# Block-sparse attention with a gated FFN on one Trainium2 core: which tensor goes through the crossbar DMA, q and k of three batches or the normalised attention output

## Chip, core and metric

The kernel runs on one core of a Trainium2 chip. The metric is device time in microseconds (us) of one execution; less is better. The kernel before takes 306.27 us, the median of three runs (305.6 to 307.56).

## What is computed

Attention over 4 batches, 8 heads, 768 tokens and 64 elements a head, with a mask of 32x32 blocks (first and last block row and column, the diagonal and its neighbours, three sampled blocks a row), and then a gated FFN over the 3072 tokens:

```python
scores = scale * np.matmul(q, k.transpose(0, 1, 3, 2))
...
scores = np.where(mask, scores, -1000000000.0)
...
attn = attn / (np.sum(attn, axis=-1, keepdims=True) + 1e-09)
return np.matmul(attn, v).astype(np.float32)
...
x = np.ascontiguousarray(attn_out.transpose(0, 2, 1, 3)).reshape(B * S, H * D)
...
gate = 1.0 / (1.0 + np.exp(-(x @ w_gate)))
val = x @ w_val
return (gate * val @ w_out).astype(np.float32)
```

x is 3072x512; w_gate and w_val are 512x1536, w_out is 1536x512. Inputs and output are float32; the kernel computes on float16.

## The kernel before, in words

**Units.** The work is cut into 12 units, numbered n (L601): batch b from 0 to 3, and within a batch three runs of 256 query tokens, u from 0 to 2. In each unit the 8 heads are taken as 4 pairs p (class `Pair`), two heads of 64 elements filling 128 partitions. A pair has 3 steps (class `Step`), each of 256 keys: scores on TensorE (L406, into one of two PSUM tiles of kind "s"), exp on ScalarE (L416), a product with the mask on VectorE (L422). Then come the product with v (L445, 24 matmuls into one of four PSUM banks of kind "m"; a column of ones in `vex` gives the row sums), and `norm` on VectorE (L455, L457), which divides and writes `x16`, 128 tokens by (2 token tiles, 2 heads, 64).

**x^T.** The FFN wants x with its 512 columns on the partitions. So each pair's `x16` is turned: `turn` (L464) makes two 128x128 transposes on TensorE into an "m" bank, and `evac` (L472) copies the bank into `xT` (four buffers, `XB`) on VectorE or ScalarE. `Pair.xt` (L487) plans both.

**FFN.** Class `Ffn`: for each of 12 column groups, `f` runs 8 matmuls (L532, gate and value into one "m" bank), tanh on ScalarE (L543), the gating on VectorE (L548). `y` (L566) runs 12 matmuls (L571) for each of two token tiles; ScalarE scales the result (L582) and SyncE's queue stores it (L589). The first `f` of a unit needs all four pairs of x^T.

**q and k.** Scores want q and k with the 64 elements of a head on the partitions. For batch 0, `prep` (L321) copies a head pair side by side into `pr` on VectorE (L329), turns it with up to six TensorE transposes into an "m" bank (L338), and copies the bank into `qT` or `kT` (L345). For batch 1, `pair_up` (L360) copies the pairs on VectorE (L364) into `kp` or `qp`, and `xbar` (L371) turns a whole batch of k or of q with one transposing DMA on SyncE's queue (L375). For batches 2 and 3 `pair_load` (L619) loads each head straight into the paired layout with 16 DMAs on GpSimd's queue (L622), followed by the same `xbar`. v is loaded in the other layout and copied into `vex` by `vcopy` (L382, L384).

**Order.** Nothing is issued in the order of the loops. Every piece is a task in `Plan` (L54), with the engines that can do it and a guessed cost, its dependencies, an earliest time `at`, and the PSUM banks that it takes and frees. `Plan.run` (L69) plays these guesses forward: whenever an engine is free it takes the ready task that was added first (so a task added late is still taken early when the engine has nothing older that is ready). The order that comes out is written into the program. On the chip each engine goes through its own list in that order, and waits on semaphores. A task's results count as ready at its end plus a lag: 0.25 for TensorE, 0.06 for ScalarE and VectorE, 16.0 for a DMA unless the task gives its own (L59). `land` (L261) holds guessed landing times of the first loads; those of batch 1 are 44.8, 48.9 and 53.0 us by the code's `DMA_RATE` for k, q and v. The loads of batches 2 and 3 have no such time: they count as landed a lag after they were issued. That lag is 55.0 in the kernel before (L661).

The main loop (L706 to L734) adds the tasks of unit n in six slots `sl`: two steps of scores; `y` of unit n-2 in slots 0 and 1, three `f` of unit n-1 in slots 2 to 5; products with v in slots 0, 2, 3 and 5, so that the fourth pair of unit n-1 comes in slot 0 of unit n; `xt` in slots 0, 1, 3 and 4; and, in units with u of 1 or 2, one entry of `preps`, the queue that `later(b)` (L627) fills for the next batch. `later(b + 1)` is called at the first unit of batch b (L708), `later(1)` after unit 0.

Of the kernel before, what the change touches and what calls it, by code (L numbers as in the profile page):

```python
# [13 lines left out]
f16 = mybir.dt.float16  # L14
# [6 lines left out]
B, H, S, D = 4, 8, 768, 64  # L21
BLK = 32
NB = S // BLK
NT = S // 128
NP = H // 2
# [5 lines left out]
UQ = 256  # L31
NU = S // UQ
PE, ACT, DVE, DMA = "PE", "ACT", "DVE", "DMA"
DMA_RATE = 0.385
XB, PB, VB = 4, 4, 5
# [86 lines left out]
def kernel(  # L122
# [43 lines left out]
    wo = sing.tile([128, NF, DM], f16)  # L166
    q16 = [sing.tile([128, H, NT, D], f16, name=f"q16_{r}") for r in range(2)]
    k16 = [sing.tile([128, H, NT, D], f16, name=f"k16_{r}") for r in range(2)]
    qp = sing.tile([128, NP, NT, 2, D], f16, name="qp")
    kp = sing.tile([128, NP, NT, 2, D], f16, name="kp")  # L170
    v16 = [sing.tile([128, H, NT, D], f16, name=f"v16_{r}") for r in range(2)]
    vex = [sing.tile([128, H, NT, D + 1], f16, name=f"vex{r}") for r in range(2)]
    qT = [sing.tile([128, NP, S], f16, name=f"qT{r}") for r in range(2)]
# [3 lines left out]
    def load_heads(dst, src, b, h0, h1, t0=0, t1=NT):  # L177
        nc.gpsimd.dma_start(  # L178
            dst[b % 2][:, h0:h1, t0:t1, :],
            src[b, h0:h1].rearrange("h (p t) d -> p h t d", t=NT)[:, :, t0:t1, :],  # L180
        )
# [70 lines left out]
    def ring(nm, bufs):  # L252

        i = len(used[nm]) - bufs
        return [used[nm][i]] if i >= 0 else []
# [65 lines left out]
    def prep(src, dst, b, p, t0, t1, deps, at):  # L321

        bank = Bank("m")
        box = []

        def pair(eng):
            pr = work.tile([128, NT, 2, D], f16, tag="pr", bufs=PB, name="pr")
            box.append(pr)
            nc.vector.tensor_copy(  # L329
                pr[:, t0:t1, :, :],  # L330
                src[b % 2][:, 2 * p : 2 * p + 2, t0:t1, :].rearrange(
                    "a h t d -> a t h d"
                ),
            )

        def turn(eng):
            for t in range(t0, t1):
                nc.tensor.transpose(  # L338
                    m16(bank.slot)[:, (t - t0) * 128 : (t - t0 + 1) * 128],
                    box[0][:, t, :, :],  # L340
                    ident,
                )

        def evac(eng):
            copy(  # L345
                eng,
                dst[b % 2][:, p, t0 * 128 : t1 * 128],
                m16(bank.slot)[:, 0 : (t1 - t0) * 128],
            )

        n = t1 - t0
        a = plan.add([(DVE, 0.15 + 0.035 * n)], pair, ring("pr", PB) + loaded[b], at=at)
        copies[b].append(a)
        c = plan.add([(PE, 0.058 * n)], turn, [a], take=[bank])
        used["pr"].append(c)
        return plan.add(
            [(DVE, 0.14 + 0.07 * n), (ACT, 0.18 + 0.1 * n)], evac, [c] + deps, free=[bank]
        )

    def pair_up(src, dst, b, p, deps, at):  # L360


        def go(eng):
            nc.vector.tensor_copy(  # L364
                dst[:, p, :, :, :],
                src[b % 2][:, 2 * p : 2 * p + 2, :, :].rearrange("a h t d -> a t h d"),
            )

        return plan.add([(DVE, 0.36)], go, deps, at=at)

    def xbar(src, dst, b, deps):  # L371


        def go(eng):
            nc.sync.dma_start_transpose(  # L375
                dst[b % 2].rearrange("a p (t n) -> a (p t) n", n=128),
                src.rearrange("a p t h d -> a (p t h d)"),
            )

        return plan.add([(DMA, 0.01)], go, deps, lag=10.0)  # L380

    def vcopy(b, p, deps, at):  # L382
        def go(eng):
            nc.vector.tensor_copy(  # L384
# [44 lines left out]
    class Pair:  # L429
# [23 lines left out]
        def norm(self, eng):  # L453
            rz = work.tile([128, 2, 2, 1], f32, tag="rz", bufs=3, name="rz")
            nc.vector.reciprocal(rz, self.acc[:, :, :, D : D + 1])  # L455
            self.x16 = work.tile([128, 2, 2, D], f16, tag="x16", bufs=4, name="x16")
            nc.vector.tensor_tensor(  # L457
                self.x16,
                self.acc[:, :, :, 0:D],
                rz.broadcast_to([128, 2, 2, D]),  # L460
                op=ALU.mult,
            )
# [16 lines left out]
        def value(self):  # L479
            a = plan.add([(PE, 0.8)], self.pv, self.products + [vdone[self.b, self.p]],  # L480
                         take=[self.bank])
            used["P"].append(a)
            read["pv", self.b, self.p] = [a]
            self.normed = plan.add([(DVE, 0.6)], self.norm, [a] + ring("x16", 4),
                                   free=[self.bank])

        def xt(self):  # L487
            c = plan.add([(PE, 0.12)], self.turn, [self.normed], take=[self.bank2])
            used["x16"].append(c)
            deps = [used["xT"][self.n - XB]] if self.n >= XB else []  # L490
            xdone[self.n].append(
                plan.add([(DVE, 0.29), (ACT, 0.37)], self.evac, [c] + deps,
                         free=[self.bank2])
            )

    def scores(run):


        def mm(eng):
            for pr, st in run:  # L500
                st.qk()

        deps = [
            x for pr, st in run for x in kdone[pr.b, pr.p] + qdone[pr.b, pr.p, pr.u]
        ]
        a = plan.add([(PE, 0.1 + 0.22 * len(run))], mm, deps, take=[st.bank for pr, st in run])
        for pr, st in run:
            read["qk", pr.b, pr.p] = [a]
            i = NP * pr.n + pr.p - VB
            old = [used["P"][i]] if i >= 0 else []  # L510
            e = plan.add([(ACT, 0.98)], st.exp, [a] + old, free=[st.bank])
            pr.products.append(plan.add([(DVE, 0.66)], st.mul, [e] + masks[st.j, st.u]))
# [89 lines left out]
    xTs = [[] for _ in units]  # L602
    xdone = [[] for _ in units]
    ffn = [Ffn(n) for n in range(len(units))]
    masks, kdone, qdone, vdone, read, turned_b = {}, {}, {}, {}, {}, {}
    preps, valued, turned = deque(), deque(), deque()

    def prep_k(b, p, at=0.0):
        kdone[b, p] = [prep(k16, kT, b, p, 0, NT, [], at)]

    def prep_q(b, p, at=0.0, t0=0, t1=NT):
        d_ = [prep(q16, qT, b, p, t0, t1, [], at)]
        for u in range(t0 // 2, t1 // 2):
            qdone[b, p, u] = d_

    def prep_v(b, p, at=0.0):
        vdone[b, p] = vcopy(b, p, read.get(("pv", b - 2, p), []), at)

    def pair_load(dst, src, b):  # L619
        for p in range(NP):  # L620
            for a in range(2):
                nc.gpsimd.dma_start(  # L622
                    dst[:, p, :, a, :],
                    src[b, 2 * p + a].rearrange("(n t) d -> n t d", t=NT),
                )

    def later(b):  # L627
        kr = [x for p in range(NP) for x in read.get(("qk", b - 2, p), [])]
        if b == 1:
            for nm, src, dst, dT, done in (  # L630
                ("k", k16, kp, kT, kdone),
                ("q", q16, qp, qT, qdone),
            ):
                ups = []
                for p in range(NP):
                    preps.append(
                        lambda p=p, nm=nm, src=src, dst=dst, ups=ups: ups.append(
                            pair_up(src, dst, b, p, [], land[nm, "next"])
                        )
                    )  # L640

                def turn(nm=nm, dst=dst, dT=dT, ups=ups):
                    turned_b[nm, b] = xbar(dst, dT, b, ups + kr)
                    for p in range(NP):
                        kdone[b, p] = [turned_b["k", b]]
                        for u in range(NU):
                            qdone[b, p, u] = [turned_b.get(("q", b))]

                preps.append(turn)
        else:  # L650

            def load(eng):
                pair_load(kp, k, b)
                pair_load(qp, q, b)
                load_heads(v16, v, b, 0, H)

            ld = plan.add(
                [(DMA, 0.01)],
                load,
                [turned_b["k", b - 1], turned_b["q", b - 1]] + copies[b - 2],  # L660
                lag=55.0,  # L661
            )
            loaded[b].append(ld)
            turned_b["k", b] = xbar(kp, kT, b, [ld] + kr)
            turned_b["q", b] = xbar(qp, qT, b, [ld] + kr)
            for p in range(NP):
                kdone[b, p] = [turned_b["k", b]]
                for u in range(NU):
                    qdone[b, p, u] = [turned_b["q", b]]
        for p in range(0, NP, 2):  # L670
            at = land["v", "next"] if b == 1 else 0.0
            preps.append(lambda p=p, at=at: [prep_v(b, p + i, at) for i in range(2)])

    def do(queue, fn):
        if queue:
# [99 lines left out]
```

## Time and profile before

The profile is of one execution that took 306.27 us, of which 304.5 us are the span from the first to the last instruction.

| | |
|---|---|
| profiled execution / its span | 306.27 / 304.5 us |
| TensorE busy | 291.4 us, 96% |
| VectorE, ScalarE busy | 200.9 us, 210.7 us |
| GpSimd busy | 48.5 us |
| TensorE clock granted | 0.997 in the mean |
| transposes of x on TensorE (L466) | 96, two a pair |
| transposes of q and k on TensorE (L338) | 48, batch 0 |
| transposing DMAs (L375) | 6, of 768 KB |

PE is TensorE's matmuls, PEld its weight loads, DVE VectorE, ACT ScalarE, POOL GpSimd, SP SyncE. A line of a timeline gives the start, the time from start to end of a merged run of instructions, and the instructions. Matmuls overlap, so what a group costs TensorE is read from the start of the group to the start of the next, not from its busy time. "m" and "s" in the profile are the PSUM tiles of the two kinds.

### The profile page before, as it was taken

How to read it: one execution, taken by the hardware profiler on the slowest of the kernel's cores; microseconds unless marked ns; L12 is line 12 of the kernel's file. 1: busy time of each engine (PE TensorE's matmuls, PEld its weight loads, DVE VectorE, ACT ScalarE, POOL GpSimd, SP SyncE). 2: the span in 40 equal slices, each digit the busy share in tenths (PEclk: the TensorE clock that was granted, in tenths of full speed). 3: DMA queues.
4: the chain of work that ended last, by engine and by line, in shares of the span. 5: the costliest groups of instructions: out<-in, count | busy, mean ns of one | idle time of the engine just before them, and what ended most of it. 6: DMA issues, size and time to landing. Idle time of an engine off the chain costs nothing.

```text
span 304.5 us, 7858 instructions
## 1 busy us (share of the span) xinstructions
PE 291.4 (96%) x3326; PEld 209.6 (69%) x3326; DVE 200.9 (66%) x474; ACT 210.7 (69%) x340; POOL 48.5 (16%) x65
## 2 busy tenths in 40 slices
PE   3978999999999999999999999999999999999994
PEld 1355785786786786786686686687687687687771
DVE  4669878876676678676676577576576577576240
ACT  3669986776776776776776776776776776774431
POOL 8943000494000059200000000000000000000000
PEclk9999999999999999999999999999999999999998
DMA  7999999999500699930100580100100100100101
GB/s 100 181 203 202 206 204 183 223 160 131 128 1 2 158 154 124 154 74 2 71 2 0 113 168 1 71 2 2 69 2 2 69 2 4 69 2 2 69 2 70
DMA packets 62768, 25.75 MB, mean 85 GB/s; under 512 B 45812, under 2 KB 59660, under 8 KB 62732
## 3 DMA queue, kind: packets, MB, share of 16 engines
q0 software_dynamic: 40400, 14.16, 40.8%
q1 hardware_dynamic: 22332, 11.09, 15.0%
q8 instruction: 26, 0.43, 0.6%
q14 instruction: 10, 0.08, 0.1%
HBM read 28.39 MB, written 6.29 MB: 114 GB/s over the span
## 4 chain that ended last, share of the span: by engine, by line
PE 93%; ACT 2%; DMA 1%; DVE 1%; issue 1%; POOL 1%; POOLq 0%
PE m L532 42%; PE m L571 21%; PE s L406 13%; PE m L445 13%; PE m L466 2%; DMA v<-in_v_dram 1%; ACT pt L416 1%; PE m L303 1%; PE m L338 1%; ACT mask L225 1%; DVE pt L422 0%; DVE kT L227 0%; POOL k L178 0%; POOL q L178 0%; ACT ysb L582 0%
## 5 line engine op out<-in xcount | busy, mean ns | idle before, releaser
L416 ACT ACTIVATE pt<-s 128x1024 f16<-128x1024 f32 x144 | 140.1, 1026 | 4.6 <-PE s L406 3.7
L422 DVE TENSOR_TENSOR pt<-pt,mask 128x1024 f16<-128x1024 f16 x144 | 97.2, 687 | 38.8 <-ACT pt L416 38.4
L532 PE MATMUL m<-xT,wg 128*128 128x256 f16 x576 | 86.7, 273 | 0.0
L532 PE MATMUL m<-xT,wv 128*128 128x256 f16 x576 | 86.4, 273 | 0.0
L543 ACT ACTIVATE th<-m 128x256 f32<-128x256 f32 x144 | 54.6, 390 | 43.8 <-PE m L532 36.0
L548 DVE SCALAR_TENSOR_TENSOR ht<-th,m 128x256 f16<-128x256 f32 x144 | 57.3, 418 | 16.4 <-ACT th L543 14.8
L571 PE MATMUL m<-wo,ht 128*128 128x512 f16 x288 | 66.0, 379 | 0.0
L532 PEld LDWEIGHTS <-wv 128*128 128x128 f16 x576 | 56.3, 98 | 6.5
L532 PEld LDWEIGHTS <-wg 128*128 128x128 f16 x576 | 51.3, 97 | 12.5 <-issue 7.2
L445 PE MATMUL m<-vex,pt 128*128 128x65 f16 x1152 | 46.5, 196 | 1.8 <-ACT mask L225 1.6
L445 PEld LDWEIGHTS <-pt 128*128 128x128 f16 x1152 | 42.6, 99 | 7.6 <-issue 5.3
L571 PEld LDWEIGHTS <-ht 128*128 128x128 f16 x288 | 26.6, 98 | 30.7 <-issue 2.1
L406 PE MATMUL s<-qT,kT 64*128 64x256 f16 x576 | 47.1, 279 | 0.6 <-DVE qT L227 0.3
L582 ACT ACTIVATE ysb<-m 128x512 f32<-128x512 f32 x24 | 14.3, 597 | 35.3 <-PE m L571 35.3
L406 PEld LDWEIGHTS <-kT 64*128 64x128 f16 x576 | 22.0, 95 | 15.8 <-issue 8.6
L622 POOL DMA_DIRECT2D kp<-in_k_dram x16 | 13.0, 822 | 64.1 <-DMA kT<-kp 37.9
L455 DVE RECIPROCAL rz<-m 128x4 f32<-128x4 f32 x48 | 8.7, 182 | 19.5 <-PE m L445 18.8
L457 DVE TENSOR_TENSOR x<-m,rz 128x256 f16<-128x256 f32 x48 | 20.4, 425 | 1.7
L227 DVE COPY xT<-m 128x256 f16<-128x256 f16 x31 | 9.0, 292 | 10.9 <-PE m L466 10.9
L466 PE MATMUL m<-ident,x 128*128 128x128 f16 x96 | 13.3, 221 | 0.1
L622 POOL DMA_DIRECT2D qp<-in_q_dram x16 | 13.1, 827 | 0.7 <-DVE pt L422 0.4
L466 PEld LDWEIGHTS <-x 128*128 128x128 f16 x96 | 9.0, 98 | 6.1 <-DVE x L457 0.7
(36 smaller groups left out, 71.9 us busy)
## 6 DMA issues: line engine op xcount, KB each, us to landing
out_dram<-ysb SPq DMA_DIRECT2D x24, 256.0 KB, 2.0
v<-in_v_dram POOLq DMA_DIRECT2D x3, 768.0 KB, 10.9
wg<-in_moe_w_gate_dram POOLq DMA_DIRECT2D x4, 384.0 KB, 12.7
wv<-in_moe_w_val_dram POOLq DMA_DIRECT2D x4, 384.0 KB, 13.6
wo<-in_moe_w_out_dram POOLq DMA_DIRECT2D x3, 512.0 KB, 16.7
kp<-in_k_dram POOLq DMA_DIRECT2D x16, 96.0 KB, 5.1
qp<-in_q_dram POOLq DMA_DIRECT2D x16, 96.0 KB, 4.5
k<-in_k_dram POOLq DMA_DIRECT2D x4, 192.0 KB, 5.6
```

Of the source, the lines that this page charges most:

```text
L406: nc.tensor.matmul(score[self.bank.slot][:, a, i, :], kT[b % 2][o : o + D, p, t * 128 : (t + 1) * 128], qT[b % 2][o : o + D, p, u * UQ : ( ...
L416: nc.scalar.activation(self.pt, score[self.bank.slot], AF.Exp, bias=0.0, scale=SCALE)
L422: nc.vector.tensor_tensor(self.pt, self.pt, m.unsqueeze(1).broadcast_to([128, 2, 2, UQ]), op=ALU.mult,)
L445: nc.tensor.matmul(self.acc[:, s, a, :], self.steps[t // 2].pt[:, a, t % 2, s * 128 : (s + 1) * 128], vex[self.b % 2][:, 2 * self.p + a, t ...
L457: nc.vector.tensor_tensor(self.x16, self.acc[:, :, :, 0:D], rz.broadcast_to([128, 2, 2, D]), op=ALU.mult,)
L466: nc.tensor.transpose(m16(self.bank2.slot)[:, s * 128 : (s + 1) * 128], self.x16[:, s, :, :], ident,)
L532: nc.tensor.matmul(pg[:, i, :], w[:, c, f * 128 : (f + 1) * 128], xTs[self.n][0][:, c, :], start=(c == 0), stop=(c == 3),)
L543: nc.scalar.activation(th, spare[bank.slot][:, 0:UQ], AF.Tanh, bias=0.0, scale=0.5)
L548: nc.vector.scalar_tensor_tensor(self.ht[:, f, :], in0=box[0], scalar=1.0, in1=spare[bank.slot][:, UQ : 2 * UQ], op0=ALU.add, op1=ALU.mult,)
L571: nc.tensor.matmul(spare[bank.slot], self.ht[:, f, s * 128 : (s + 1) * 128], wo[:, f, :], start=(f == 0), stop=(f == NF - 1),)
L582: nc.scalar.activation(ysb, spare[bank.slot], AF.Copy, bias=0.0, scale=0.5)
L622: nc.gpsimd.dma_start(dst[:, p, :, a, :], src[b, 2 * p + a].rearrange("(n t) d -> n t d", t=NT),)
```

## The change

It swaps what goes through the crossbar. q and k of batches 1 to 3 are prepared as in batch 0 (`prep`: VectorE copy, six TensorE transposes, copy out of PSUM; 24 calls of `prep`, 144 transposes). `pair_up`, `xbar`, `pair_load`, `qp` and `kp` go. In units 1 to 11, `Pair.xt` gives each pair's `x16` to one transposing DMA on SyncE's queue that writes `xT` directly (44 DMAs of 64 KB), with a planned lag of 3.0; unit 0 keeps TensorE. `x16` gets six buffers in place of four. The loads of batches 2 and 3 are three DMAs each; they wait only for the copies out of the same buffers two batches earlier, and have the plan's lag of 16.0.

```diff
-            self.x16 = work.tile([128, 2, 2, D], f16, tag="x16", bufs=4, name="x16")
+            self.x16 = work.tile([128, 2, 2, D], f16, tag="x16", bufs=6, name="x16")
...
+        def xbar(self, eng):
+            if not xTs[self.n]:
+                xTs[self.n].append(
+                    work.tile([128, NP, UQ], f16, tag="xT", bufs=XB, name="xT")
+                )
+            nc.sync.dma_start_transpose(
+                xTs[self.n][0][:, self.p, :].rearrange("a (s n) -> a s n", s=2),
+                self.x16.rearrange("a s h d -> a (s h d)"),
+            )
+
         def xt(self):
+            if self.n > 0:
+                deps = [used["xT"][self.n - XB]] if self.n >= XB else []
+                c = plan.add([(DMA, 0.05)], self.xbar, [self.normed] + deps, lag=3.0)
+                used["x16"].append(c)
+                xdone[self.n].append(c)
+                return
             c = plan.add([(PE, 0.12)], self.turn, [self.normed], take=[self.bank2])
...
     def prep_k(b, p, at=0.0):
-        kdone[b, p] = [prep(k16, kT, b, p, 0, NT, [], at)]
+        kdone[b, p] = prep(k16, kT, b, p, 0, NT, read.get(("qk", b - 2, p), []), at)
...
-    def pair_load(dst, src, b):
+    def later(b):
+        if b > 1:
+
+            def load(eng):
+                for src, dst in ((k, k16), (q, q16), (v, v16)):
+                    load_heads(dst, src, b, 0, H)
+
+            loaded[b].append(plan.add([(DMA, 0.01)], load, copies[b - 2]))
         for p in range(NP):
-            for a in range(2):
-                nc.gpsimd.dma_start(
-                    dst[:, p, :, a, :],
-                    src[b, 2 * p + a].rearrange("(n t) d -> n t d", t=NT),
-                )
-
-    def later(b):
...
-            ld = plan.add(
-                [(DMA, 0.01)],
-                load,
-                [turned_b["k", b - 1], turned_b["q", b - 1]] + copies[b - 2],
-                lag=55.0,
-            )
...
-            turned_b["k", b] = xbar(kp, kT, b, [ld] + kr)
-            turned_b["q", b] = xbar(qp, qT, b, [ld] + kr)
...
+            for nm, fn in (("k", prep_k), ("q", prep_q), ("v", prep_v)):
+                preps.append(
+                    lambda fn=fn, p=p, at=land[nm, "next"] if b == 1 else 0.0: fn(b, p, at)
+                )
```

More of the change, by code (lines that the diff above doesn't have):

```diff
@@ L168 @@
     k16 = [sing.tile([128, H, NT, D], f16, name=f"k16_{r}") for r in range(2)]
-    qp = sing.tile([128, NP, NT, 2, D], f16, name="qp")
-    kp = sing.tile([128, NP, NT, 2, D], f16, name="kp")
     v16 = [sing.tile([128, H, NT, D], f16, name=f"v16_{r}") for r in range(2)]
@@ L358, in prep @@
         )
[L360 to L366, printed above, removed]
-            )
[L369 to L377, printed above, removed]
-            )
-        return plan.add([(DMA, 0.01)], go, deps, lag=10.0)
     def vcopy(b, p, deps, at):
@@ L483, in value @@
             read["pv", self.b, self.p] = [a]
-            self.normed = plan.add([(DVE, 0.6)], self.norm, [a] + ring("x16", 4),
+            self.normed = plan.add([(DVE, 0.6)], self.norm, [a] + ring("x16", 6),
                                    free=[self.bank])
-        def xt(self):
+        def xbar(self, eng):
[7 more added lines that the diff above has]
+            )
+        def xt(self):
+            if self.n > 0:
[4 more added lines that the diff above has]
+                return
             c = plan.add([(PE, 0.12)], self.turn, [self.normed], take=[self.bank2])
@@ L501, in mm @@
                 st.qk()
-        deps = [
-            x for pr, st in run for x in kdone[pr.b, pr.p] + qdone[pr.b, pr.p, pr.u]
-        ]
+        deps = [x for pr, st in run for x in (kdone[pr.b, pr.p], qdone[pr.b, pr.p, pr.u])]
         a = plan.add([(PE, 0.1 + 0.22 * len(run))], mm, deps, take=[st.bank for pr, st in run])
@@ L604 @@
     ffn = [Ffn(n) for n in range(len(units))]
-    masks, kdone, qdone, vdone, read, turned_b = {}, {}, {}, {}, {}, {}
+    masks, kdone, qdone, vdone, read = {}, {}, {}, {}, {}
     preps, valued, turned = deque(), deque(), deque()
     def prep_k(b, p, at=0.0):
-        kdone[b, p] = [prep(k16, kT, b, p, 0, NT, [], at)]
+        kdone[b, p] = prep(k16, kT, b, p, 0, NT, read.get(("qk", b - 2, p), []), at)
     def prep_q(b, p, at=0.0, t0=0, t1=NT):
-        d_ = [prep(q16, qT, b, p, t0, t1, [], at)]
+        d_ = prep(q16, qT, b, p, t0, t1, read.get(("qk", b - 2, p), []), at)
         for u in range(t0 // 2, t1 // 2):
@@ L627, in later @@
-    def later(b):
[L628 to L655, printed above, removed]
-            ld = plan.add(
-                [(DMA, 0.01)],
-                load,
-                [turned_b["k", b - 1], turned_b["q", b - 1]] + copies[b - 2],
-                lag=55.0,
-            )
-            loaded[b].append(ld)
-            turned_b["k", b] = xbar(kp, kT, b, [ld] + kr)
-            turned_b["q", b] = xbar(qp, qT, b, [ld] + kr)
[L666 to L672, printed above, removed]
```

## The prediction

> **What bounds the kernel now.** I read the page first: busy shares and the chain that ended last.
>
> ```profile
> span 304.5 us, 7858 instructions
> PE 291.4 (96%) x3326; PEld 209.6 (69%) x3326; DVE 200.9 (66%) x474; ACT 210.7 (69%) x340; POOL 48.5 (16%) x65
> PEclk9999999999999999999999999999999999999998
> PE 93%; ACT 2%; DMA 1%; DVE 1%; issue 1%; POOL 1%; POOLq 0%
> ```
>
> TensorE carries the chain, at full granted clock, while VectorE and ScalarE idle a third of the time. A busy share can hide waiting inside a stage, so next I took the timeline of TensorE over one steady unit.
>
> ```profile
> 231.45 0.60 PE L532 MATMUL m<-xT,wv 128*128 128x256 f16 x4
> 231.98 0.61 PE L406 MATMUL s<-qT,kT 64*128 64x256 f16 x8
> 232.52 0.95 PE L445 MATMUL m<-vex,pt 128*128 128x65 f16 x24
> 233.31 2.75 PE L571 MATMUL m<-wo,ht 128*128 128x512 f16 x12
> 235.90 0.28 PE L466 MATMUL m<-ident,x 128*128 128x128 f16 x2
> 236.11 0.61 PE L406 MATMUL s<-qT,kT 64*128 64x256 f16 x8
> 236.65 2.76 PE L571 MATMUL m<-wo,ht 128*128 128x512 f16 x12
> 239.25 0.28 PE L466 MATMUL m<-ident,x 128*128 128x128 f16 x2
> 239.46 0.61 PE L406 MATMUL s<-qT,kT 64*128 64x256 f16 x8
> 240.00 0.94 PE L445 MATMUL m<-vex,pt 128*128 128x65 f16 x24
> 240.78 0.60 PE L532 MATMUL m<-xT,wg 128*128 128x256 f16 x4
> ```
>
> From start to start: four L532 0.44, 24 L445 0.78, 12 L571 2.59, eight scores 0.54 and 0.09 more ahead of them after another kind of matmul (231.45 to 231.98 is 0.53, not 0.44). Two L466 ahead of scores take 0.21, of which 0.09 is that lead, so a pair's transposes cost about 0.11; where y follows them (281.55 to 281.66 in the same view) they also cost 0.11. A unit by these prices: 24 x 0.44 + 2 x 2.59 + 4 x 0.78 + 6 x 0.63 + 4 x 0.11 = 23.1 us; the first y of successive units starts at 210.38 and 233.47 in the chain, 23.1 apart. So TensorE has no hole to put work into: what is added is paid, what is removed is earned.
>
> Last, the loads of batch 1 on GpSimd's queue, the view of v's landings (the maximum is batch 1's, k's and q's are 19.7 and 21.6) and VectorE's timeline, for when data arrives against when it is asked for.
>
> ```profile
> 26.39 0.89 POOL L178 DMA_DIRECT2D k<-in_k_dram  x1 [0.66 <-DMA wv<-in_moe_w_val_dram]
> 28.34 0.88 POOL L178 DMA_DIRECT2D q<-in_q_dram  x1 [1.06 <-DMA wg<-in_moe_w_gate_dram]
> 30.32 0.88 POOL L178 DMA_DIRECT2D v<-in_v_dram  x1 [1.10 <-DMA wv<-in_moe_w_val_dram]
> ...
> DMA to landing us min/median/max: 4.2/6.3/23.8
> ```
> ```profile
> 28.81 0.69 DVE L329 COPY pr<-q 128x512 f16<-128x512 f16 x2
> ...
> 50.80 1.16 DVE L364 COPY qp<-q 128x768 f16<-128x768 f16 x4
> ...
> 58.00 0.87 DVE L548 SCALAR_TENSOR_TENSOR ht<-th,m 128x256 f16<-128x256 f32 x2
> 58.78 0.42 DVE L384 COPY vex<-v 128x768 f16<-128x768 f16 x1
> ```
>
> k, q and v of batch 1 land at 46.1, 49.9 and 54.1: full rate, 4.0 apart. All four qp copies ran at 50.8, though three of them were added for the unit whose first y starts at 48.67: VectorE's list takes late tasks as soon as the plan holds them ready.
>
> **The change, part by part.**
>
> *TensorE, transposes.* Removed: 44 pairs x 0.11 = 4.8 us. Added: 24 x 6 = 144 transposes. The row for these, L338, is there only in batch 0: eight take 0.54 from 29.61 to 30.15, less the 0.09 lead 0.056 each; L466 gives 0.055. Taking 0.055: 144 x 0.055 = 7.9. Net +3.1. At 0.053 or 0.060 the net is +2.8 or +3.8. Units without preparation go to 22.7, the six with it to 24.0.
>
> The Trainium skill, TensorE: Matmul & The Clock Gate, Part 4, gives a transpose about 275 ns in a kernel; counted so, the net 56 would be 15.4 us. This trace shows a duration of 0.22 to 0.28 us too, but in a stream the next group starts after 0.055 each, and that price decides.
>
> *VectorE, ScalarE, PSUM.* Added: 24 pair copies of 0.36 (L329), 24 copies out of PSUM of 0.55 on VectorE or 0.80 on ScalarE. Removed: 8 pair_up copies of 0.35, 44 evac of 0.29 or 0.37. At worst, all added work on VectorE, a steady unit of 24.0 holds 15.4 + 4 x 0.91 = 19.1 us of VectorE: hidden beside TensorE. "m" banks: 44 uses gone, 24 longer ones added. I take 0; up to 0.3 us in each of six units if a late copy holds a bank.
>
> *The x^T DMAs.* Each is issued by SyncE when norm is done. The trace has no 64 KB transpose. From below: a 256 KB store lands in 2.0. From above: the 768 KB transposes land in 7.2. Of these, 3.5 to 6.2 is the issue, for 24 tiles of 128x128, so two tiles take 0.3 to 0.5, and some 2.9 remain after the issue: 3.3 us, nearer the store. Cover: the fourth pair is the tight one. Its norm ends at 234.16 (VectorE's timeline, 233.73 + 0.43), the first f starts at 240.78, or 240.56 without the two turns: 6.4 us, filled by two y. In the last unit, 279.80 to 284.1: 4.3. Taken as 0; at 7.2 it is 0.8 x 10 + 2.9 = 11 us. On SyncE's queue a store that waits for its y can stand ahead of a DMA, or the reverse; the fourth pair's norm ends 1.9 before ScalarE starts the unit's first scaling (236.10), so the order fits. Stores that come later delay nobody before the end.
>
> The Trainium skill, DMA: Bandwidth & Descriptors, Rules for kernel authors, speaks against this: many small transfers should be one large one, since below 64 KB one pays mostly overhead; its fit would give 2.15 us each, 95 us for all 44. By the cover above that is latency nobody waits for.
>
> *Loads of batches 2 and 3.* Removed on GpSimd: 32 issues of 0.82, hidden. What matters is when VectorE's list asks. The load of batch 2 now depends only on batch 0's copies, the last of which end at 29.5; the plan calls it landed 16 later, near 46. On the chip it queues behind batch 1: at 4.0 each after 54.1, k, q, v of batch 2 land near 58.1, 62.1 and 66.1. Batch 2's copies of k and q also wait in the plan for earlier `pr` buffers (the turns of batch 1's third and fourth pairs, some 52 to 57), its v copies for the last product with batch 0's v of the same pair (first pair: norm starts at 56.23). So I expect these copies in VectorE's list from about 54 on. v decides: the first VectorE gap after that product is 58.78 now; six turns more (6 x 0.33) and four turns of x fewer (0.44) make it 60.3; v lands at 66.1. VectorE stands for up to 5.8 us, in two or three waits, and behind it the mask products, norms and gatings of that unit. TensorE runs on until its four "m" banks are full, say two f (1.75). Loss: 4.0. Bounds: 0, if the plan places these copies after 66, where unit 4's tasks would put them; 8.4, if v is asked for at 56.23 + 1.5 and TensorE stops at once. Nothing nearer prices it; I take 4.0, about the middle. Batch 3 is loaded some 20 us later with nothing ahead of it in the queue: 0.
>
> *Sum.* Span 304.5 + 3.1 + 4.0 = 311.6; the 1.77 around it in the profiled execution, whose time equals the median, makes 313.4.
>
> **The rivals.**
>
> 1. *No late load.* The copies stand late enough in VectorE's list, or TensorE has the slack. 306.27 + 3.1 = 309.4. For it: TensorE's list seldom has a hole, so turns may stay in the order of their units, and `pr` buffers then come free late. Against: the qp copies at 50.8, taken early.
> 2. *The x^T DMA is exposed.* It lands after 6.4 us because loads up to 78 share the engines, or the queue is blocked. At 7.2 it costs 11: 320.4 with no late load. For: kT's issue took 6.2 at 48.6, beside loads, and 3.7 at 102.2. Against: the bytes are a twelfth.
> 3. *The late load is worse*: the upper bound of 8.4, 317.8, or more where k and q wait in turn and the banks fill early.
> 4. *Faster.* The turns of q and k cost less than those of x. It decides at 4.8/144 = 33 ns each; at the 32 ns of an L445 matmul (0.78/24) the change would gain 0.2, and for 303.2, 1% faster, they would have to cost 12 ns each. Against: every run of L338 and L466 at full pace shows 55.
>
> **How the numbers follow.** Within 1% is 303.2 to 309.3, about what a measurement can tell from no change. Chances: forecast (a loss of 1 to 8 us) 0.52; rival 1 0.24; rival 2 0.11; rival 3 beyond 8 us 0.09; rival 4 0.04. Predicted 313.4. The range from 309.0 to 318.5 takes in the forecast, rival 1 nearly whole, and the late load's upper bound; left out are rival 4, and most of rivals 2 and 3, 0.2 together. Rival 1 sits on the border, so half of it counts as within 1%: slower 0.52 + 0.11 + 0.09 + 0.12 = 0.84, same 0.12, faster 0.04.
>
> **What would show it.** Transposes: 8 of x and 192 of q and k, 0.055 from start to start; units at 22.7 and 24.0. Transposing DMAs: 44, landing in some 3.3 us, and no wait of TensorE on xT. Late load: VectorE waiting on DMAs of k, q or v between 54 and 70, holes in TensorE just after, a unit 2 of 28 us rather than 24. It is wrong if unit 2 shows no such wait, if TensorE waits for x^T DMAs at each unit's first f, or if units with preparation exceed 24 us by a wait for banks.

## The result and the profile after

The changed kernel takes 314.37 us (median of four runs, 313.92 to 315.12) against 306.72 for the kernel before on the same chip: ratio 1.0254, 95% interval 1.0211 to 1.0298. The forecast was 313.4 within 309.0 to 318.5. Line numbers of the changed kernel are smaller by 2 to 24. On TensorE, L336 turns q and k, L382 makes the scores, L421 is the product with v, L522 and L561 are `f` and `y`. On VectorE, L327 is the copy of `prep`, L360 that of `vcopy`, L398 the product with the mask, L431 and L433 are `norm`, L538 is the gating. L392 is exp and L572 the scaling on ScalarE; L468 issues x^T's DMAs.

The page of the changed kernel, the lines that answer to those of before:

```profile
span 313.3 us, 8030 instructions
PE 295.7 (94%) x3382; PEld 211.8 (68%) x3382; DVE 200.7 (64%) x470; ACT 216.0 (69%) x340; POOL 25.9 (8%) x37
PEclk9999999979999999999999999999999999999999
PE 82%; DMA 11%; ACT 4%; DVE 1%; issue 1%; POOL 0%; DVEq 0%; POOLq 0%
```

TensorE has 56 more instructions, its net 56 transposes. New are DMAs on the chain, 11% after 1%. That share counts a load's whole flight, so it is no measure of what was lost: e1_lag45 below has 12% there. New too is a slice, the ninth of 40 (62.7 to 70.5 us), in which the granted clock is below 0.8. VectorE's timeline there (start, time of the run, instructions, in brackets the idle time before them and what ended it):

```profile
53.50 0.35 DVE L327 COPY pr<-q 128x768 f16<-128x768 f16 x1
59.67 0.36 DVE L327 COPY pr<-k 128x768 f16<-128x768 f16 x1 [5.82 <-DMA k<-in_k_dram]
59.94 1.28 DVE L398 TENSOR_TENSOR pt<-pt,mask 128x1024 f16<-128x1024 f16 x2
61.15 1.16 DVE L360 COPY vex<-v 128x768 f16<-128x768 f16 x4
64.33 0.36 DVE L327 COPY pr<-q 128x768 f16<-128x768 f16 x1 [2.02 <-DMA q<-in_q_dram]
...
68.06 0.36 DVE L360 COPY vex<-v 128x768 f16<-128x768 f16 x1 [0.63 <-DMA v<-in_v_dram]
```

Batch 2's first copy of k stands in VectorE's list right behind batch 1's last, some 50 us before unit 4, and waits 5.8 us for its load; the first copy of q waits 2.0. The two mask products of 59.94 had long been ready: the exps that they read ended at 54.1 and 55.0 (ScalarE's timeline, two exps from 53.05). TensorE's timeline shows what hung on them:

```profile
57.59 0.29 PE L421 MATMUL m<-vex,pt 128*128 128x65 f16 x4
60.69 0.81 PE L421 MATMUL m<-vex,pt 128*128 128x65 f16 x20 [2.81 <-DVE pt L398]
...
63.18 0.61 PE L382 MATMUL s<-qT,kT 64*128 64x256 f16 x8
65.90 0.62 PE L522 MATMUL m<-xT,wg 128*128 128x256 f16 x4 [2.11 <-DVE x L433]
66.33 1.04 PE L522 MATMUL m<-xT,wv 128*128 128x256 f16 x4
67.16 1.53 PE L421 MATMUL m<-vex,pt 128*128 128x65 f16 x24
68.50 1.04 PE L522 MATMUL m<-xT,wg 128*128 128x256 f16 x4
69.33 0.81 PE L522 MATMUL m<-xT,wv 128*128 128x256 f16 x4
69.98 0.60 PE L522 MATMUL m<-xT,wg 128*128 128x256 f16 x4
```

Two holes, 2.8 and 2.1 us, and the view of TensorE's waits has no other behind the first f. The first ends with a mask product that L421 reads; the second with `norm`, which reads the bank that L522 then fills. After the second, four L522 take 0.83 from start to start (66.33 to 67.16), where they took 0.44, and 24 L421 take 1.34 in place of 0.78. The view by stretches says why; its column after the engines is the granted clock:

```profile
65.00:66.00 1.00, 0.10 (x1) 0.10 (x1) 0.97 (x4) 0.56 (x1) 0.00 (x0) 1.00 1.32 205
66.00:67.00 1.00, 1.00 (x8) 0.77 (x7) 1.00 (x3) 0.00 (x0) 0.00 (x0) 0.67 1.30 200
67.00:68.00 1.00, 1.00 (x17) 0.94 (x16) 0.43 (x2) 0.39 (x1) 0.00 (x0) 0.50 1.32 205
69.00:70.00 1.00, 1.00 (x8) 0.73 (x7) 0.97 (x4) 0.00 (x0) 0.00 (x0) 0.63 1.33 212
70.00:71.00 1.00, 1.00 (x13) 0.91 (x11) 0.91 (x3) 0.38 (x1) 0.00 (x0) 1.00 2.00 142
```

Behind the holes the clock falls to half for some 3 us, and 1.6 us more are lost (0.39 + 0.56 + 0.39 + 0.21 over the groups from 66.33 to 69.98). Elsewhere the units run as priced; the same view for unit 3, which prepares nothing, and unit 4, which prepares batch 2, from y to y:

```profile
80.59:103.24 22.65, 22.65 (x267) 16.19 (x265) 15.03 (x34) 16.78 (x27) 0.00 (x0) 1.00 0.13 37
103.24:127.22 23.98, 23.98 (x293) 17.77 (x290) 16.49 (x38) 17.57 (x29) 0.00 (x0) 1.00 0.12 35
```

And the view of xT:

```profile
L468 SPq DMA_TRANSPOSE xT<-x x44: 1168/1170/1907, 35.2 to 289.6; - x44
DMA to landing us min/median/max: 2.3/2.3/6.4
```

TensorE never waits for a DMA of x^T in this kernel. The two traces can be compared from the first f on TensorE to the last scaling on ScalarE, first before, then after:

```profile
31.30 0.61 PE L532 MATMUL m<-xT,wg 128*128 128x256 f16 x4
300.11 0.60 ACT L582 ACTIVATE ysb<-m 128x512 f32<-128x512 f32 x1 [1.99 <-PE m L571]
```
```profile
31.19 0.61 PE L522 MATMUL m<-xT,wg 128*128 128x256 f16 x4
309.81 0.60 ACT L572 ACTIVATE ysb<-m 128x512 f32<-128x512 f32 x1 [1.99 <-PE m L561]
```

They differ by 9.8 us: 4.9 in the holes, 1.6 at the lower clock, and 3.3 left for the transposes. The spans differ by 8.8, because after the last scaling 3.5 us follow here and 4.4 before, and the first f came 0.1 sooner.

### The profile page after: what moved, and what is told of

Read it like the earlier page. It is cut to its first block, busy times and chain, and to the rows that moved or that the text cites. A ratio compares the mean times of both kernels' runs of the same rounds, so it can differ in the third digit from the quotient of the medians.

```text
span 313.3 us, 8030 instructions
## 1 busy us (share of the span) xinstructions
PE 295.7 (94%) x3382; PEld 211.8 (68%) x3382; DVE 200.7 (64%) x470; ACT 216.0 (69%) x340; POOL 25.9 (8%) x37
## 4 chain that ended last, share of the span: by engine, by line
PE 82%; DMA 11%; ACT 4%; DVE 1%; issue 1%; POOL 0%; DVEq 0%; POOLq 0%
PE m L522 38%; PE m L561 18%; PE m L421 11%; PE s L382 11%; DMA q<-in_q_dram 9%; ACT pt L392 3%; PE m L336 3%; DMA v<-in_v_dram 2%; PE m L301 1%; ACT mask L223 0%; DVE pt L398 0%; ACT xT L223 0%; POOL k L176 0%; POOL q L176 0%; DVE ht L538 0%
## 5 line engine op out<-in xcount | busy, mean ns | idle before, releaser
L392 ACT ACTIVATE pt<-s 128x1024 f16<-128x1024 f32 x144 | 140.0, 1024 | 4.2 <-PE s L382 3.9
L398 DVE TENSOR_TENSOR pt<-pt,mask 128x1024 f16<-128x1024 f16 x144 | 97.9, 688 | 54.7 <-ACT pt L392 54.4
L522 PE MATMUL m<-xT,wg 128*128 128x256 f16 x576 | 87.2, 274 | 2.1 <-DVE x L433 2.1
L533 ACT ACTIVATE th<-m 128x256 f32<-128x256 f32 x144 | 54.5, 389 | 49.4 <-PE m L522 42.0
L522 PE MATMUL m<-xT,wv 128*128 128x256 f16 x576 | 87.1, 274 | 0.0
L538 DVE SCALAR_TENSOR_TENSOR ht<-th,m 128x256 f16<-128x256 f32 x144 | 56.2, 417 | 17.7 <-ACT th L533 17.2
L561 PE MATMUL m<-wo,ht 128*128 128x512 f16 x288 | 65.8, 379 | 0.0
L522 PEld LDWEIGHTS <-wg 128*128 128x128 f16 x576 | 50.7, 98 | 16.5 <-issue 11.4
L522 PEld LDWEIGHTS <-wv 128*128 128x128 f16 x576 | 56.7, 98 | 6.8
L421 PE MATMUL m<-vex,pt 128*128 128x65 f16 x1152 | 47.1, 197 | 4.6 <-DVE pt L398 3.0
L421 PEld LDWEIGHTS <-pt 128*128 128x128 f16 x1152 | 44.1, 100 | 8.8 <-issue 4.7
L561 PEld LDWEIGHTS <-ht 128*128 128x128 f16 x288 | 26.8, 98 | 30.9 <-issue 2.1
L382 PE MATMUL s<-qT,kT 64*128 64x256 f16 x576 | 46.8, 278 | 0.6 <-DVE qT L225 0.3
L572 ACT ACTIVATE ysb<-m 128x512 f32<-128x512 f32 x24 | 14.3, 597 | 33.4 <-PE m L561 33.4
L382 PEld LDWEIGHTS <-kT 64*128 64x128 f16 x576 | 21.9, 95 | 20.9 <-issue 16.2
L433 DVE TENSOR_TENSOR x<-m,rz 128x256 f16<-128x256 f32 x48 | 20.4, 424 | 1.7
L336 PE MATMUL m<-ident,pr 128*128 128x128 f16 x192 | 16.9, 230 | 0.4 <-DVE pr L327 0.4
L431 DVE RECIPROCAL rz<-m 128x4 f32<-128x4 f32 x48 | 8.7, 182 | 11.6 <-PE m L421 11.3
L336 PEld LDWEIGHTS <-pr 128*128 128x128 f16 x192 | 13.2, 103 | 4.2 <-DVE pr L327 1.3
L327 DVE COPY pr<-k 128x768 f16<-128x768 f16 x16 | 5.7, 363 | 7.2 <-DMA k<-in_k_dram 6.8
L327 DVE COPY pr<-q 128x768 f16<-128x768 f16 (+2 forms) x20 | 6.4, 331 | 2.2 <-DMA q<-in_q_dram 2.2
L360 DVE COPY vex<-v 128x768 f16<-128x768 f16 x16 | 5.6, 364 | 3.2 <-DMA v<-in_v_dram 3.2
```

The lines of the kernel that those rows point to most:

```text
L327: nc.vector.tensor_copy(pr[:, t0:t1, :, :], src[b % 2][:, 2 * p : 2 * p + 2, t0:t1, :].rearrange("a h t d -> a t h d"),)
L336: nc.tensor.transpose(m16(bank.slot)[:, (t - t0) * 128 : (t - t0 + 1) * 128], box[0][:, t, :, :], ident,)
L382: nc.tensor.matmul(score[self.bank.slot][:, a, i, :], kT[b % 2][o : o + D, p, t * 128 : (t + 1) * 128], qT[b % 2][o : o + D, p, u * UQ : ( ...
L392: nc.scalar.activation(self.pt, score[self.bank.slot], AF.Exp, bias=0.0, scale=SCALE)
L398: nc.vector.tensor_tensor(self.pt, self.pt, m.unsqueeze(1).broadcast_to([128, 2, 2, UQ]), op=ALU.mult,)
L421: nc.tensor.matmul(self.acc[:, s, a, :], self.steps[t // 2].pt[:, a, t % 2, s * 128 : (s + 1) * 128], vex[self.b % 2][:, 2 * self.p + a, t ...
```

## The experiments

The theory: most of the loss is batch 2's late load, through VectorE's list; the rest is TensorE's price of 0.055 us a transpose; x^T's DMAs are hidden. Rivals: the preparation of q and k costs more than its transposes; the DMAs of x^T cost TensorE time. Runs e1 to e4 were on one chip (306.02 for the kernel before), e5 to e7 on another (306.31).

**e1_lag45: the late load taken away**

```diff
-            loaded[b].append(plan.add([(DMA, 0.01)], load, copies[b - 2]))
+            loaded[b].append(plan.add([(DMA, 0.01)], load, copies[b - 2], lag=45.0))
```

> The changed kernel, with the planned lag of the loads of batches 2 and 3 at 45.0 in place of 16.0; nothing else. The late-load theory says: in the changed kernel's trace VectorE waits 5.8 us for k and 2.0 us for q of batch 2, TensorE stands 2.8 and 2.1 us behind that and then runs at half its clock from 66 to 69 us, some 6.5 us in all. With the copies planned after the landing all of it goes: about 308.5 us (ratio to the kernel before 1.003 to 1.010), no wait of VectorE on DMAs of batch 2, no hole in TensorE between 57 and 71 us, unit 2 about 24 us. The rival, that the transposes of q and k cost more than 0.055 us each through PSUM banks and copies, says 313 us or more, with the lag making no difference. The rival that TensorE waits for the x^T DMAs says the same.

308.33 us, ratio 1.0075 (1.0053 to 1.0098). One number in the planner is worth most of the change's loss. From 48 to 72 us:

```profile
48.00:72.00 24.00, 23.66 (x276) 17.54 (x273) 18.41 (x43) 17.49 (x30) 2.63 (x3) 1.00 1.31 203
```

0.34 us idle in place of 4.9, full clock. The theory's numbers came; both rivals, which allowed the lag no effect, fall. From first f to last scaling (29.95 to 302.54) this trace is 3.8 us over before.

**e3_all_tensor: no transposing DMA at all**

```diff
 (against e1_lag45)
-            if self.n > 0:
+            if False:
```

> The lag of 45.0 as in e1_lag45, and x^T of all units on TensorE as in the kernel before: no transposing DMA at all. If a transpose costs its 0.055 us of TensorE and nothing else matters, it is 4.8 us over e1_lag45, about 313.4 us, and 7.9 us less the first unit's rounding over the kernel before (ratio 1.022). If the x^T DMAs cost TensorE something in e1_lag45, the distance to it is smaller, or the sign turns.

313.89 us, ratio 1.0257 (1.0235 to 1.0279). Over the kernel before that is 7.9 us for 144 transposes, 0.055 each; over e1_lag45 it is 5.6 for 88, 0.063 each. Part of the 5.6 lies ahead of the first f, where both kernels do the same work: e1_lag45's profiled execution reached it 1.15 us sooner (29.95, 31.10). From first f to last scaling (307.93) the two traces differ by 4.2, 0.048 each. So x^T through the crossbar is worth about what its transposes cost TensorE.

**e5_turn_twice: the price of a transpose**

```diff
 (against e1_lag45)
-            for t in range(t0, t1):
+            for t in list(range(t0, t1)) * (2 if b > 1 else 1):
```

> e1_lag45 with the turn of q and k of batches 2 and 3 made twice over, into the same place: 96 more TensorE transposes, nothing else. If a transpose costs what lies between two starts, 0.055 us: 5.3 us more than e1_lag45, about 313.6 us. If its duration counts (0.22 us) 21 us more; by the figure of the Trainium skill, TensorE: Matmul & The Clock Gate, Part 4, of about 275 ns, an estimate of 26 us more.

313.82 us, ratio 1.0262 (1.0233 to 1.029), 5.5 us over e1_lag45 for 96: 0.057 each. From first f to last scaling (30.59 to 308.03) it is 4.9, 0.051 each. What counts in a stream is the distance of two starts. The 275 ns that the Trainium skill (TensorE: Matmul & The Clock Gate, Part 4) gives is near the duration in the traces, 0.22 to 0.28 us, but no measure of what such a stream costs.

**e6_lag32: between the two lags**

```diff
 (against e1_lag45)
-load, copies[b - 2], lag=45.0))
+load, copies[b - 2], lag=32.0))
```

> The changed kernel with the planned lag of the loads at 32.0, between its own 16.0 and the 45.0 of e1_lag45. The plan then calls batch 2 landed near 62 us, and on the chip k, q and v land at 59.5, 64.2 and 68. The late-load theory says that the wait for k goes, and that one of some 1 to 3 us stays for q, one of up to 4 for v: between e1_lag45 and the changed kernel, 309 to 312 us, and less of TensorE's clock lost. If only the order of TensorE's list had mattered, not the landing, it is the same as e1_lag45.

312.76 us (311.14 to 314.77), ratio 1.0225 (1.0173 to 1.0276): longer than expected, and too spread to rank against the changed kernel. In the profiled execution, the shortest of the four, k and q are in time, and v is the one that is late, first in VectorE's timeline, then in TensorE's:

```profile
68.98 0.36 DVE L360 COPY vex<-v 128x768 f16<-128x768 f16 x1 [3.47 <-DMA v<-in_v_dram]
```
```profile
71.47 0.60 PE L522 MATMUL m<-xT,wg 128*128 128x256 f16 x4 [2.34 <-DVE ht L538]
```

TensorE loses 2.3 us to a wait of 3.5, at full clock. The other three executions had a mean granted clock of 0.989 to 1.0; the longest, 314.77, had the lowest. That a clock drop in some of them makes the spread fits, but only the shortest has a trace, so it is not shown.

**e4_twice_xbar: x^T's DMA doubled**

```diff
 (against e1_lag45)
+            for _ in range(2):
                 nc.sync.dma_start_transpose(
```

> e1_lag45 with every x^T DMA issued twice in a row, the same bytes to the same place: the second lands some 1.2 to 2.3 us after the first, so 3.5 to 4.6 us after norm in place of 2.3. The theory that x^T's way through the crossbar is hidden with 6.4 us to spare (4.3 in the last unit) says no change against e1_lag45, within 0.5 us. If TensorE's first f of a unit waits for it, 11 units lose 1.2 to 2.3 us each: 13 to 25 us more.

325.58 us, ratio 1.0642 (1.0615 to 1.0669), 17 us over e1_lag45. My expectation was wrong. TensorE's waits:

```profile
PE m L523 <- DMA xT<-x: 13.7, 3, 6.9
```
```profile
64.01 0.37 PE L523 MATMUL m<-xT,wg 128*128 128x256 f16 x1 [5.88 <-DMA xT<-x]
71.29 0.37 PE L523 MATMUL m<-xT,wg 128*128 128x256 f16 x1 [6.90 <-DMA xT<-x]
```

Two of the three, 5.9 and 6.9 us, stand at the first f after unit 1 (to 64.01 and 71.29); the third, 0.9, at the last unit; the units between show none. I had doubled the median landing of 2.3. But in unit 1 the loads are still running, and there one DMA of x^T lands after 5.9 to 6.4, and the second is held until the first has landed. SyncE stands meanwhile (44 waits for a DMA of x^T, 68.5 us in all), so the four pairs queue up: their eight issues run from 36.3 to 66.6, where the four of e1_lag45 run from 34.0 to 49.0. Of the 17 us, 13.7 are these waits, 1.3 the low clock behind them (71.46 to 74.44, start to start), and 2.2 lie ahead of the first f (32.23 here), which the edit does not touch. That 17 lies within the 13 to 25 that I gave to eleven exposed units is luck: one unit lost nearly all of it. In the changed kernel the fourth pair of unit 1 is issued at 49.1 and lands near 55.3; its reader starts at 56.70. So beside loads the cover has 1.4 us left, not the 3 that I had reckoned. That the DMAs of x^T cost TensorE time is refuted for the changed kernel by its own trace, yet it is close by.

**e2_both_xbar: the other half of the change alone**

In the kernel before, x^T of units 1 to 11 goes through the crossbar as in the change's diff (`xbar` and the branch in `xt`, six `x16` buffers), while q and k stay there too.

> The kernel before with only the other half of the change: x^T of units 1 to 11 by a crossbar DMA for each pair, while q and k of batches 1 to 3 stay on the crossbar too. If x^T's DMAs are hidden and the 88 transposes taken off TensorE are worth 0.055 us each, it gains 4.8 us: 301.9 us (0.984). The rival: SyncE's queue then holds two kinds, and a 768 KB transpose, 3.5 to 6.2 us in the issue, stands ahead of the fourth pair's x^T three or more times; each could cost TensorE 2 to 5 us, and a clock drop behind it: 304 to 312 us.

310.26 us, ratio 1.0135 (1.0111 to 1.0159): slower, though 88 transposes have left TensorE and none came. SyncE's queue and TensorE:

```profile
48.33 8.01 SPq L375 DMA_TRANSPOSE kT<-kp  x1
56.46 1.17 SPq L492 DMA_TRANSPOSE xT<-x  x1
```
```profile
54.77 0.50 PE L548 MATMUL m<-xT,wg 128*128 128x256 f16 x3
58.77 0.27 PE L548 MATMUL m<-xT,wg 128*128 128x256 f16 x1 [3.50 <-DMA xT<-x]
```

The 768 KB transpose of k holds the queue for 8 us in its issue; the fourth pair's x^T stands behind it. f has done three of its four gate matmuls (one a pair) and waits 3.5 us for the last. At batch 3's k the same costs 2.3:

```profile
198.97 0.27 PE L548 MATMUL m<-xT,wg 128*128 128x256 f16 x1 [2.27 <-DMA xT<-x]
```

Each hole has a low-clock stretch behind it. The sum: -4.8 + 5.8 leaves 3.2 of the measured 4.2, and the groups behind the two holes (60.08 to 63.54, 199.51 to 203.77), read from start to start, lose 1.6 each to the clock, as in the changed kernel.

**e7_split_both: the same with the queue in order**

Three things change together: the transposes of k and q are split by head pair, the plan is given the queue time of every issue, and batch 1's are held back to 54 us, with the loads' lag at 48. Some lines of it:

```diff
 (against e2_both_xbar)
-        return plan.add([(DMA, 0.01)], go, deps, lag=10.0)
+        return plan.add([(DMA, 1.5)], go, deps, at=at, lag=6.0)
...
-                dst[b % 2].rearrange("a p (t n) -> a (p t) n", n=128),
-                src.rearrange("a p t h d -> a (p t h d)"),
+                dst[b % 2][:, p, :].rearrange("a (t n) -> a t n", n=128),
+                src[:, p].rearrange("a t h d -> a (t h d)"),
...
-                c = plan.add([(DMA, 0.05)], self.xbar, [self.normed] + deps, lag=3.0)
+                c = plan.add([(DMA, 1.2)], self.xbar, [self.normed] + deps, lag=3.0)
```

> e2_both_xbar with SyncE's queue put in order: the transposing DMAs of k and q are split by head pair (24 of 192 KB in place of 6 of 768 KB), each planned with 1.5 us of the queue and x^T's with 1.2, batch 1's held back to 54 us, and the loads' lag at 48.0, so that in SyncE's list all of them stand behind the fourth pair's x^T of a unit and ahead of the next unit's. If what spoiled e2_both_xbar was x^T standing behind a long transpose (3.5 and 2.3 us of TensorE, and its clock halved afterwards), then the 4.8 us of transposes taken off TensorE are now earned: about 301.9 us (0.985 of the kernel before). If transposing DMAs of x beside loads are late by themselves, or the next unit's scores wait for k and q, 304 to 310 us.

300.91 us, ratio 0.9833 (0.9808 to 0.9858): 5.4 us under the kernel before and so also under the changed kernel, which took 1.0254 of that. TensorE's one wait of this kind:

```profile
PE m L546 <- DMA xT<-x: 0.8, 1, 0.8
```

From first L522 (30.68) to last scaling (295.46) it is 4.0 us under before: 4.8 earned, 0.8 lost at unit 1, where the loads run. Splitting by itself saves no queue time: one issue of 192 KB takes 1.2 us on quiet DMA engines, so four take 5.0 where one of 768 KB took 3.6. What is gone is x^T standing behind them; how much each of the three did was not tried.

## Why the prediction was right, and where it was not

- *TensorE is full, so transposes are paid and earned at 0.055.* Held: units of 22.65 and 23.98 us against 22.7 and 24.0, and 0.055 to 0.063 a transpose by the medians of e3_all_tensor and e5_turn_twice, 0.048 to 0.056 by their traces from first f to last scaling. The net of 3.1 measured 2.3 (1.6 to 3.0) by e1_lag45's ratio and 3.8 by its trace from first f to last scaling; e1's profiled execution reached its first f 1.35 us sooner than that of before, so these differ by what lies ahead of that f.
- *VectorE, ScalarE and PSUM banks at 0.* Held: no hole in the steady units.
- *x^T's DMAs at 0.* Held for the result. The two sizes were off: the issue takes 1.17 us, not 0.3 to 0.5, the landing 2.3, not 3.3; and beside loads it is 5.9 to 6.4, at the edge of the cover. The issue cannot be scaled down by the number of tiles: 64, 192 (e7_split_both) and 768 KB take at least 1.17, 1.2 and 3.5 us. I had one landing for all places.
- *Late load at 4.0.* The mechanism held, from the place to what hangs on it; the size was short: 4.9 us of holes and 1.6 at half clock, 6.5. k, q and v landed at 59.6, 64.2 and 68.0 (issued at 32.71, 34.64 and 36.94, with the longest landings in the views of their tiles, 26.9, 29.6 and 31.1), later than the 58.1, 62.1 and 66.1 that I had. "v decides" failed: k, asked for at 53.9, shifted everything, and by then v was nearly there (0.63). Only with k and q in time does v decide, as e6_lag32 shows. I had VectorE stand for up to 5.8 us in all and 1.75 of that covered; it stood 5.82 for k, 2.02 for q and 0.63 for v, 8.5, and 3.6 were covered. TensorE stopped first not because its four banks were full but for a mask product; only the second hole ended with a bank coming free. The clock was missing altogether. Unit 2 took 31.7 us from y to y (48.89 to 80.59), not 28: beside the 6.5, it held 42 transposes of q and k, not 24.
- *Batch 3 at 0.* Held, but not for my reason. Its loads of k and q were issued at 54.5 and 55.4, while batch 2's were still in flight, and not 20 us later with nothing ahead of them. No copy had to wait for them: after 70 us VectorE waits for no load.
- 313.4 lies nearer to 314.37 than the parts do, and that is in part luck. The profiled execution took 315.12, 1.7 over the forecast: 2.5 from the late load and 0.2 from the transposes, less 1.0 outside the stretch from first f to last scaling. The median of the four executions is 0.75 lower again.
- Rivals: no late load (309.4) is e1_lag45, 308.33, not the changed kernel. The exposed x^T did not happen here, and happened in e2_both_xbar and e4_twice_xbar. Faster had no support: it needed transposes of less than 0.033, and the lowest reading is 0.048.

## What to carry to other kernels

A planner that guesses when a load lands writes that guess into the order of an in-order engine: an early guess makes the engine stand, with ready work behind it. So read each load's landing from the trace and set its lag by that, for each place, because the same DMA can take nearly three times as long beside other loads (2.3 against 6.2 us for x^T here). When work moves to a DMA queue, give the planner the queue time of every issue on it, and keep short transfers that somebody waits for ahead of long ones.

## What the runs showed of the hardware

- Short holes of TensorE cost more than themselves. After 2.8 and 2.1 us idle with some 3 us of work between, the granted clock was 0.50 for two slices of 1 us and 0.67 and 0.63 in the ones beside them, which cost 1.6 us. In e2_both_xbar single holes of 3.5 and 2.3 did the same (0.54 to 0.60 and 0.50 in the stretches after), while the hole of 2.3 in e6_lag32's profile did not (1.00 throughout). The Trainium skill, TensorE: Matmul & The Clock Gate, Why this matters for your kernels, warns of idle gaps over some 3 us; the 3.5 agrees with it, the drop after 2.3 shows that a shorter one can be enough, and what sets the two of 2.3 apart stays open: it was not tried.
- A transposing DMA holds SyncE's queue for longer when it is larger, though not in proportion, and for longer beside loads: 1.17 us for 64 KB, 1.2 to 2.1 for 192 KB (e7_split_both), 3.5 to 6.2 for 768 KB in the kernel before, 8.0 in e2_both_xbar beside loads.
- 64 KB from SBUF to SBUF through the crossbar land in 2.3 us on quiet DMA engines and 5.9 to 6.4 us beside 200 GB/s of loads (unit 1 of the changed kernel and of e4_twice_xbar).
